# Agent attention and a SoLU feed-forward on one core: the small softmax is transposed two tiles at a time and split into high and low parts behind the transpose

## The chip, the cores and the metric

The kernel runs on one core of one Trainium2 chip. A core has TensorE (PE, matrix products, with a separate weight load PEld), VectorE (DVE), ScalarE (ACT), GpSimd (POOL), and SyncE (SP), whose queue issues all DMAs of this kernel. They run side by side, each through its own list of instructions in a fixed order, and wait for one another by semaphores. The metric is the device time of one execution in microseconds; the time before is the median of three.

## What is computed

Four batches of 12608 rows of 128 columns go through an agent attention with 49 agents and then, all rows together, through a feed-forward of width 1024:

```python
def sm(a, b):
    s = scale * (a @ b.transpose(0, 2, 1))
    e = np.exp(s - s.max(-1, keepdims=True))
    return e / (e.sum(-1, keepdims=True) + 1e-09)
agent_v = sm(agents, k) @ v
x = (sm(q, agents) @ agent_v).reshape(B * S, D)
h = x @ w_in
e = np.exp(h - max(h)); solu = h * e / (sum(e) + 1e-09)
ln = (solu - mean(solu)) / np.sqrt(var(solu) + 1e-06) * g_ln
return ln @ w_out
```

## The kernel before

The rows are cut into 396 tiles of 128, 99 to a batch. Three kinds of work run mixed.

**The agent pass** of a batch (`phase_a`) goes over keys and values in 13 chunks and ends with two matrices `mh` and `ml`, the high and the low part of agent_v times w_in. It runs beside the tiles of the batch before it, so the last batch has none beside it; that of the first batch stands alone at the start, together with the unpacking of the weights.

**The small softmax** of the queries over the 49 agents (`phase_b`) takes units of eight tiles, and in them groups of up to four: 25 groups in a batch, 24 of four tiles and one of three. TensorE makes the logits (`b0`, L647), DVE and ACT turn them into exponentials and the reciprocal of their sum (`b1` to `b3r`). Then, for each group, `b4` on POOL multiplies (L676), copies the result rounded to the fp32r format into columns 0 to 48 of the tile's 128 columns of `pack` (L678), and puts the rest, the low part, into columns 64 to 112 (L680). `b5` transposes each tile's 128 columns by itself into a PSUM bank (L687), and `b6` on ACT copies the bank into `pT` (L692). In `pT` the high part lies in rows 0 to 48 and the low part in rows 64 to 112; `mh` and `ml` hold the same rows twice, so one product takes both parts.

**The tile loop**: `c_h` multiplies a tile's 128 columns of `pT` with `mh` and `ml` into one of two double banks `ph` (L730, four matmuls a tile); DVE takes the maximum (`c_max`, L734), ACT the exponential (`c_exp`, L744), DVE the product with h (`c_u`, L749), ACT the squares (`c_sq`, L755). `c_t` transposes the 1024 columns of the result in two halves of four (L762). A half is then split into a high and a low part in one of two ways: where the table `DIR` (by tile number modulo four, and half) says direct, ACT writes the high part (L777) and DVE subtracts it from PSUM (L786); otherwise ACT copies the half to `uT` (L781) and POOL makes both parts (L790, L794). The last two tiles are direct throughout. `c_w` makes the last product for two tiles at once in 24 matmuls (L810). POOL computes the scale of four tiles (`c_rstd`), which DMAs take to DRAM (`dr`, four small ones, L851) and back to all partitions (`rB`, L852); `c_fin` on DVE multiplies with it (L875) and `c_out` stores (L891).

**What sets the order.** `Plan` is a list scheduler that runs when the program is built: each piece of work is an `op` with an engine, an assumed duration, a due time in tiles and the pieces that it needs; the planner gives the engine that can start first the piece due first among those that can start at about that time. The due times are tile numbers plus constants (`BD0` to `DWL`). The planner's order is fixed for TensorE, ACT, DVE and POOL (the last loop of the kernel); SP's is not, and follows from the tile framework. Transposes, logits, agent products and last products share four PSUM banks `px`: `take` takes one, `free` names the piece after which it is given back. `pT` has eight buffers (`PTB`), each of the two `pack` one.

Of the kernel before, what the change touches and what calls it, by code (L numbers as in the profile page):

```python
# [9 lines left out]
F32 = mybir.dt.float32  # L10
F32R = mybir.dt.float32r
# [3 lines left out]
ALU = mybir.AluOpType  # L15
# [10 lines left out]
class Plan:  # L26
# [15 lines left out]
    def op(self, eng, fn, cost, due, deps=(), take=False, free=None, after=(), kind=1, shy=0.0):  # L42
        o = Op()
        o.kind, o.shy = kind, shy
        o.eng, o.fn, o.cost, o.due, o.take, o.free = eng, fn, cost, due, take, free
        o.deps, o.outs, o.end, o.bank = [d for d in deps if d is not None], [], None, None
        o.left = 0
        for d in o.deps + [d for d in after if d is not None]:
            if d.end is None:
                o.left += 1  # L50
                d.outs.append(o)
        if not o.left:
            self.push(o)
        return o
# [71 lines left out]
def kernel(  # L126
# [11 lines left out]
    nc = tc.nc  # L138
    B, C, N = qT.shape
    A = agT.shape[2]  # L140
    DF = w_in.shape[1]
    P = 128
    NF = DF // P
    HW = 512
    GT = 4
# [3 lines left out]
    AP2 = 64  # L149
    ETE = "AD"  # L150
    CPR = -1.98
    UTB = 4
    DIR = {(1, 0), (1, 1), (3, 1)}
    LGC = 8
    UB = 8
    TD = 2
    WC = 4

    BD0 = 13.69
    BD1 = 15.3  # L160
    BD2 = 9.96
    BD3 = -17.37
    BD4 = 0.17
    BD5 = 5.85
    DH = -3.24
    DMX = -8.66
    DEX = 0.61
    DU_ = -1.62
    DSQ = 20.92
    DT = -0.42  # L170
    DEV = -8.39
    DLD = 1.53
    DSP = -1.16
    DW = 3.3
    DR = 1.58
    DF_ = 5.14
    OUTD = -5.86
    OUTC = -74.58
# [4 lines left out]
    VLAG = 0.25  # L183
    PTB = 8
    SHY = -2.99
    DHR = -4.68
    DHL = -5.42
    DMXR = 10.02
    DMXL = 15.46
# [11 lines left out]
    DLDL = 26.96  # L201
    DSPR = -6.09
    DSPL = 14.43
    DWR = 2.46
    DWL = -0.21
    RBL = 6.0
    ASTART = -3.67
# [6 lines left out]
    const = ctx.enter_context(tc.tile_pool(name="const", bufs=1))  # L214
# [3 lines left out]
    bpool = ctx.enter_context(tc.tile_pool(name="bpool", bufs=2))  # L218
# [8 lines left out]
    ident = const.tile([P, P], F32, name="ident")  # L227
# [118 lines left out]
        ycol.append(yc)  # L346
    packs = []
    for i in range(2):
        pk = const.tile([P, GT, P], F32, name=f"pack{i}")
        nc.gpsimd.memset(pk, 0.0)  # L350
        packs.append(pk)
    logits = []
# [10 lines left out]
    op = plan.op  # L363
# [4 lines left out]
    n = len(seq)  # L368
# [247 lines left out]
    BT, B0, B4, B5, BQ, pT_op, grp_h = {}, {}, {}, {}, {}, {}, {}  # L616

    def col0(t):
        return min(t * P, N - P)
# [12 lines left out]
    groups = []  # L632

    def phase_b(k, dues, gate=()):

        b, t0, nt = units_b[k]
        r = {}
        nq = (nt + GT - 1) // GT

        def b0(j0, j1, px=None):  # L640
            if px is not None:
                r["px"] = px
            qt, px = qts[k], r["px"]
            for j in range(j0, j1):
                for h in range(0, P, AP2):
                    o = col0(t0 + j) - col0(t0) + h
                    nc.tensor.matmul(px[h : h + AP2, j * A : (j + 1) * A], qt[:, o : o + AP2], ag_sb[:, b, :A],  # L647
                                     start=True, stop=True)
            r["lg"] = px[:, : nt * A].rearrange("p (t a) -> p t a", a=A)

        def b1():
            r["mx"] = tiny.tile([P, UB], F32, tag="mx", name=f"mx{b}_{t0}")
            nc.vector.tensor_reduce(out=r["mx"][:, :nt], in_=r["lg"], op=ALU.max, axis=AX.X)

        def b1s():
            mx, lg = r.pop("mx"), r.pop("lg")
            r["e"] = logits[k % 2][:, :nt, :]
            r["d"] = r["e"][:, :, :A]
            nc.vector.tensor_tensor(out=r["d"], in0=lg, in1=mx[:, :nt].unsqueeze(2).to_broadcast([P, nt, A]),
                                    op=ALU.subtract)  # L660

        def b2():
            nc.scalar.activation(out=r["d"], in_=r["d"], func=AF.Exp, scale=SCALE)

        def b3():
            r["s"] = tiny.tile([P, UB], F32, tag="sm", name=f"sm{b}_{t0}")[:, :nt]
            nc.vector.tensor_reduce(out=r["s"], in_=r["e"], op=ALU.add, axis=AX.X)

        def b3r():
            nc.vector.reciprocal(out=r["s"], in_=r["s"])  # L670

        def b4(q):
            m = min(GT, nt - q * GT)
            sl = slice(q * GT, q * GT + m)
            pk, dv = packs[q], r["d"][:, sl, :]
            nc.gpsimd.tensor_tensor(out=dv, in0=dv, in1=r["s"][:, sl].unsqueeze(2).to_broadcast([P, m, A]),  # L676
                                    op=ALU.mult)
            nc.gpsimd.tensor_scalar(out=pk[:, :m, :A].bitcast(F32R), in0=dv, scalar1=1.0, scalar2=0.0,  # L678
                                    op0=ALU.mult, op1=ALU.add)
            nc.gpsimd.tensor_tensor(out=pk[:, :m, AP2 : AP2 + A].bitcast(F32R), in0=dv, in1=pk[:, :m, :A],  # L680
                                    op=ALU.subtract)

        def b5(q, px):
            m = min(GT, nt - q * GT)
            r["pt", q] = px
            for j in range(m):
                nc.tensor.transpose(px[:, j * P : (j + 1) * P], packs[q][:, j, :], ident)  # L687

        def b6(q):
            m = min(GT, nt - q * GT)  # L690
            pT = pTs[b, t0 // GT + q] = bpool.tile([P, GT * P], F32R, tag="pT", bufs=PTB, name=f"pT{b}_{t0}_{q}")
            nc.scalar.copy(out=pT[:, : m * P], in_=r.pop(("pt", q))[:, : m * P])  # L692

        shy = SHY if k < 4 else 0.0
        chunks = [(j, min(j + LGC, nt)) for j in range(0, nt, LGC)]
        prev, first = None, None
        for j0, j1 in chunks:
            f = (lambda px, j0=j0, j1=j1: b0(j0, j1, px)) if prev is None else (lambda j0=j0, j1=j1: b0(j0, j1))
            o = op("P", f, 0.155 * (j1 - j0), dues[0] + 0.1 * j0,
                   [BQ[k], prev, B0.get(k - 1)] + [B4.get((k - 2, q)) for q in range(2)] + list(gate), take=prev is None, kind=2, shy=shy)  # L700
            first = first or o
            prev = o
        B0[k] = prev
        d1 = op("D", b1, 0.047 + 0.0532 * nt, dues[1], [prev], shy=shy)
        d2 = op("D", b1s, 0.05 + 0.0532 * nt, dues[1] + 0.1, [d1] + [B4.get((k - 2, q)) for q in range(2)], free=first, shy=shy)
        a1 = op("A", b2, 0.098 + 0.0402 * nt, dues[2], [d2])
        d3 = op("D", b3, 0.05 + 0.0532 * nt, dues[3], [a1], shy=shy)
        d5 = op("D", b3r, 0.12, dues[3] + 0.2, [d3])
        for q in range(nq):
            g = len(groups)  # L710
            groups.append((b, t0 // GT + q))
            sc = min(GT, nt - q * GT) / GT
            old = B5.get((k - 1, q)) or B5.get((k - 2, q))
            B4[k, q] = op("G", lambda q=q: b4(q), 0.07 + 1.5 * sc, dues[4] + 2.5 * q, [d5, old])
            B5[k, q] = op("P", lambda px, q=q: b5(q, px), 0.435 * sc, dues[5] + 2.5 * q,
                          [B4[k, q], grp_h.get(groups[g - PTB]) if g >= PTB else None], take=True, shy=shy)
            pT_op[groups[g]] = op("A", lambda q=q: b6(q), 0.48 * sc, dues[5] + 2.5 * q + 0.3, [B5[k, q]], free=B5[k, q], shy=shy)
        if k + 2 < nu and k + 2 > 1:
            qload(k + 2, dues[0], [prev])

# [41 lines left out]
            nc.tensor.transpose(pt[:, kf * P : (kf + 1) * P], us[x][0][:, k0 * P : (k0 + 1) * P], ident)  # L762

    def direct(x, hf):
        return (x % GT, hf) in DIR or x >= n - TD

    def parts(x, k0, k1):
        i, j = divmod(x, 2)
# [162 lines left out]
    for x in range(n):  # L931
        b, t = seq[x]
        G, j = divmod(x, GT)
        i = x // 2
        if t % UB == 0:
            first = x
            dues = [first - z for z in (BD0, BD1, BD2, BD3, BD4, BD5)] if ku else [-99.5 + 0.05 * z for z in range(6)]
            phase_b(ku, dues, [] if ku < 2 else [mlast[0]] if ku < 4 else [])
            ku += 1
        for hf in range(2):  # L940
            H[x, hf] = op("P", F(c_h, x, hf), 0.468, at(x, DH, DHR, DHL) + 0.02 * hf,
                          [pT_op[b, t // GT], U.get(x - 2)] + mdone[b][: hf + 1], kind=0)
        grp_h[b, t // GT] = last_h[b] = H[x, 1]
        MX[x] = op("D", F(c_max, x), 1.13, at(x, DMX, DMXR, DMXL), [H[x, 0], H[x, 1]])
        EX[x] = op("A", F(c_exp, x), 1.11, at(x, DEX, DEXR, DEXL), [MX[x], U.get(x - 2), RB.get(G - 3)] + (cout if x < 2 else []))
# [40 lines left out]
        if j == GT - 1:  # L986
# [74 lines left out]
```

## Time and profile before

| | us |
|---|---|
| runs shown | 1573.73, 1576.07, 1573.48; median 1573.73 |
| the profiled execution | 1575.81 |
| its span, first to last instruction | 1574.0 |
| granted TensorE clock | 0.999 of full |
| first L730 (first product of the tile loop) | 64.9 |
| idle of DVE's L734 for TensorE's L730 | 53.3 |
| idle of POOL's L790 for ACT's L781 | 84.6 |

The profile shows one execution. The page gives each engine's busy time and its share of the span, and groups of instructions by line with count, busy time, mean duration and the idle time of the engine ahead of them. The chain of work that ended last goes back from the last instruction, at each step to what released it; its shares by line say where the time goes. A wait is put down to what came last. TensorE's matmuls overlap by a part of their length, so the length of one is read from the pieces of the chain, not from its row.

### The profile page before, as it was taken

How to read it: one execution, taken by the hardware profiler on the slowest of the kernel's cores; microseconds unless marked ns; L12 is line 12 of the kernel's file. 1: busy time of each engine (PE TensorE's matmuls, PEld its weight loads, DVE VectorE, ACT ScalarE, POOL GpSimd, SP SyncE). 2: the span in 40 equal slices, each digit the busy share in tenths (PEclk: the TensorE clock that was granted, in tenths of full speed). 3: DMA queues.
4: the chain of work that ended last, by engine and by line, in shares of the span. 5: the costliest groups of instructions: out<-in, count | busy, mean ns of one | idle time of the engine just before them, and what ended most of it. 6: DMA issues, size and time to landing. Idle time of an engine off the chain costs nothing.

```text
span 1574.0 us, 35069 instructions
## 1 busy us (share of the span) xinstructions
PE 1550.8 (99%) x12821; PEld 1381.7 (88%) x12821; DVE 1376.5 (87%) x2161; ACT 1440.1 (91%) x2740; POOL 1254.5 (80%) x1715
## 2 busy tenths in 40 slices
PE   8899999999999999999999999999999999999998
PEld 5588898998889899898899899898988989999998
DVE  6989898888998888889898888988888998989986
ACT  3599999999999999999999998999989999999996
POOL 2577888888788788787888878887878889988896
PEclk9999999999999999999999999999999999999999
DMA  9422323313123223222222232222111121111111
GB/s 370 150 88 81 96 81 95 95 59 103 62 82 100 82 88 105 91 81 74 88 68 88 88 102 88 88 88 87 49 63 53 47 69 55 62 55 49 45 42 40
DMA packets 57629, 133.65 MB, mean 85 GB/s; under 512 B 9840, under 2 KB 14064, under 8 KB 57456
## 3 DMA queue, kind: packets, MB, share of 16 engines
q1 hardware_dynamic: 57456, 131.41, 26.2%
q8 instruction: 101, 1.65, 0.4%
q14 instruction: 72, 0.59, 0.1%
HBM read 105.36 MB, written 26.02 MB: 83 GB/s over the span
## 4 chain that ended last, share of the span: by engine, by line
PE 89%; DVE 4%; ACT 3%; POOL 2%; issue 1%; DMA 0%; SPq 0%; DVEq 0%; ACTq 0%; POOLq 0%
PE px L810 33%; PE ph L730 22%; PE px L762 21%; PE px L647 3%; PE px L467 3%; PE px L418 3%; PE px L687 3%; PE px L451 1%; ACT e L744 1%; DVE u L749 1%; ACT sq L755 1%; DVE nm L734 1%; POOL uL L794 0%; ACT uT L781 0%; DVE mxp L423 0%
## 5 line engine op out<-in xcount | busy, mean ns | idle before, releaser
L794 POOL TENSOR_TENSOR uL<-uT,uH 128x1024 fp32r<-128x1024 f32 (+1 forms) x295 | 598.6, 2029 | 24.3
L734 DVE TENSOR_REDUCE nm<-ph 128x1 f32<-128x1024 f32 x396 | 480.3, 1219 | 55.3 <-PE ph L730 53.3
L749 DVE SCALAR_TENSOR_TENSOR u<-ph,e 128x1024 f32<-128x1024 f32 x396 | 481.0, 1219 | 54.2 <-ACT e L744 30.3
L755 ACT ACTIVATE sq<-u,su 128x1024 bf16<-128x1024 f32 x396 | 464.0, 1172 | 25.9 <-DVE u L749 22.8
L744 ACT ACTIVATE e<-ph,nm 128x1024 f32<-128x1024 f32 x396 | 446.3, 1132 | 28.4 <-DVE nm L734 25.0
L810 PE MATMUL px<-uL,wH 128*128 128x256 f32 x1584 | 467.2, 295 | 0.1
L810 PE MATMUL px<-uH,wH 128*128 128x256 f32 x1584 | 453.5, 286 | 2.6 <-DVE uL L786 1.4
L810 PE MATMUL px<-uH,wL 128*128 128x256 f32 x1584 | 449.4, 284 | 0.0
L762 PE MATMUL px<-ident,u 128*128 128x128 f32 x3168 | 429.4, 274 | 2.6 <-DVE u L749 0.7
L762 PEld LDWEIGHTS px<-ident,u 128*128 128x128 f32 x3168 | 355.6, 141 | 51.5 <-issue 18.7
L790 POOL TENSOR_SCALAR uH<-uT 128x1024 fp32r<-128x1024 f32 (+1 forms) x295 | 268.3, 909 | 85.7 <-ACT uT L781 84.6
L730 PE MATMUL ph<-mh,pT 128*128 128x512 f32 x792 | 326.3, 412 | 0.7 <-DVE u L749 0.4
L810 PEld LDWEIGHTS px<-uH,wH 128*128 128x128 f32 x1584 | 299.7, 189 | 15.4 <-issue 3.8
L730 PE MATMUL ph<-ml,pT 128*128 128x512 f32 x792 | 312.4, 394 | 0.0
L810 PEld LDWEIGHTS px<-uH,wL 128*128 128x128 f32 x1584 | 300.2, 189 | 9.6
L810 PEld LDWEIGHTS px<-uL,wH 128*128 128x128 f32 x1584 | 299.8, 189 | 9.0 <-issue 4.6
L781 ACT COPY uT<-px 128x512 f32<-128x512 f32 x492 | 272.9, 594 | 13.7 <-issue 3.0
L786 DVE TENSOR_TENSOR uL<-px,uH 128x512 fp32r<-128x512 f32 x300 | 200.9, 681 | 28.0 <-ACT uH L777 27.7
L777 ACT CAST uH<-px 128x512 fp32r<-128x512 f32 x300 | 170.1, 603 | 2.9 <-PE px L762 2.6
L730 PEld LDWEIGHTS ph<-mh,pT 128*128 128x128 f32 x792 | 149.2, 188 | 22.6 <-DVE u L749 4.6
L730 PEld LDWEIGHTS ph<-ml,pT 128*128 128x128 f32 x792 | 149.7, 189 | 17.1 <-DVE ml L543 0.2
L829 POOL TENSOR_TENSOR y<-x,nhalf 128x4 f32<-128x4 f32 x99 | 100.1, 1011 | 7.5
(119 smaller groups left out, 1469.2 us busy)
## 6 DMA issues: line engine op xcount, KB each, us to landing
rB<-dr SPq DMA_DIRECT2D x98, 256.0 KB
qt<-in_qT_dram SPq DMA_DIRECT2D x48, 512.0 KB
out_dram<-ob SPq DMA_DIRECT2D x95, 256.0 KB
kt<-in_kT_dram SPq DMA_DIRECT2D x36, 512.0 KB
vt<-in_v_dram SPq DMA_DIRECT2D x36, 512.0 KB
dr<-yr SPq DMA_DIRECT2D x392, 0.5 KB
kh<-in_kT_dram SPq DMA_DIRECT2D x12, 512.0 KB
vh<-in_v_dram SPq DMA_DIRECT2D x12, 512.0 KB
```

The source lines that it names most:

```text
L730: nc.tensor.matmul(ph[:, sl], lhs, bmats[b]["mh" if m == 0 else "ml"][:, sl], start=(m == 0), stop=(m == 1))
L734: nc.vector.tensor_reduce(out=nms[x], in_=phs[x], op=ALU.max, axis=AX.X, negate=True)
L744: nc.scalar.activation(out=es[x], in_=phs[x], func=AF.Exp, bias=nms.pop(x), accum_out=st[G]["S"][:, j : j + 1])
L749: nc.vector.scalar_tensor_tensor(out=u, in0=phs[x], scalar=INV, in1=es[x], op0=ALU.mult, op1=ALU.mult, accum_out=su)
L755: nc.scalar.activation(out=sq, in_=u, func=AF.Square, bias=su, scale=-float(DF), accum_out=st[G]["Q"][:, j : j + 1])
L762: nc.tensor.transpose(pt[:, kf * P : (kf + 1) * P], us[x][0][:, k0 * P : (k0 + 1) * P], ident)
L777: nc.scalar.copy(out=uH, in_=pt)
L781: nc.scalar.copy(out=rr[x][:, hf * 4 : hf * 4 + 4, :], in_=pt)
L786: nc.vector.tensor_tensor(out=uL, in0=pt, in1=uH.bitcast(F32), op=ALU.subtract)
L790: nc.gpsimd.tensor_scalar(out=uH, in0=rr[x][:, k0:k1, :], scalar1=1.0, scalar2=0.0, op0=ALU.mult, op1=ALU.add)
L794: nc.gpsimd.tensor_tensor(out=uL, in0=rr[x][:, k0:k1, :], in1=uH.bitcast(F32), op=ALU.subtract)
L810: nc.tensor.matmul(po, wt[:, kf, :], ut[:, kf, :], start=(q == 0), stop=(q == WM - 1))
```

## The change

`pack` has 64 columns a tile in place of 128, and `b4` is one multiplication on POOL that writes into it. `b5` transposes two tiles at once, so the even tile's probabilities come out in rows 0 to 48 of the bank and the odd tile's in rows 64 to 112, and a group of four needs 256 columns of the bank. `b6` on ACT copies them, rounded to fp32r, into a new SBUF tile `pn`; the new `b7` on DVE subtracts that from the bank and writes the low part beside it. The new `b8` issues four DMAs on SP that bring the parts to their rows of `pT`: for the even tiles the high part to rows 0 to 63 and the low part to rows 64 to 127, for the odd tiles the other way round. `DIR` is now by tile number modulo eight, with 5 of 16 halves direct in place of 6. The planner gets the new pieces and new constants.

```diff
-    DIR = {(1, 0), (1, 1), (3, 1)}
+    DIR = {(1, 0), (1, 1), (3, 1), (5, 1), (7, 1)}
...
-    BD1 = 15.3
+    BD1 = 8.27
...
-        pk = const.tile([P, GT, P], F32, name=f"pack{i}")
+        pk = const.tile([P, GT, AP2], F32, name=f"pack{i}")
...
-            nc.gpsimd.tensor_tensor(out=dv, in0=dv, in1=r["s"][:, sl].unsqueeze(2).to_broadcast([P, m, A]),
-                                    op=ALU.mult)
-            nc.gpsimd.tensor_scalar(out=pk[:, :m, :A].bitcast(F32R), in0=dv, scalar1=1.0, scalar2=0.0,
-                                    op0=ALU.mult, op1=ALU.add)
-            nc.gpsimd.tensor_tensor(out=pk[:, :m, AP2 : AP2 + A].bitcast(F32R), in0=dv, in1=pk[:, :m, :A],
-                                    op=ALU.subtract)
+            nc.gpsimd.tensor_tensor(out=packs[q][:, :m, :A], in0=r["d"][:, sl, :],
+                                    in1=r["s"][:, sl].unsqueeze(2).to_broadcast([P, m, A]), op=ALU.mult)
...
-            for j in range(m):
-                nc.tensor.transpose(px[:, j * P : (j + 1) * P], packs[q][:, j, :], ident)
+            for j in range(0, m, 2):
+                nc.tensor.transpose(px[:, j * AP2 : (j + 2) * AP2], packs[q][:, j : j + 2, :].rearrange("p j a -> p (j a)"),
+                                    ident)
...
         def b6(q):
+            w = (min(GT, nt - q * GT) + 1) // 2 * P
+            r["n", q] = bpool.tile([P, 2, GT // 2 * P], F32R, tag="pn", bufs=2, name=f"pn{b}_{t0}_{q}")
+            nc.scalar.copy(out=r["n", q][:, 0, :w], in_=r["pt", q][:, :w])
+
+        def b7(q):
+            w = (min(GT, nt - q * GT) + 1) // 2 * P
+            pn = r["n", q]
+            nc.vector.tensor_tensor(out=pn[:, 1, :w], in0=r.pop(("pt", q))[:, :w], in1=pn[:, 0, :w].bitcast(F32),
+                                    op=ALU.subtract)
+
+        def b8(q):
             m = min(GT, nt - q * GT)
+            pn = r.pop(("n", q))
             pT = pTs[b, t0 // GT + q] = bpool.tile([P, GT * P], F32R, tag="pT", bufs=PTB, name=f"pT{b}_{t0}_{q}")
-            nc.scalar.copy(out=pT[:, : m * P], in_=r.pop(("pt", q))[:, : m * P])
+            to = pT.rearrange("a (g i p) -> a g i p", i=2, p=P)
+            for i in range(2):
+                w = (m + 1 - i) // 2
+                r0 = i * AP2
+                for part in range(2):
+                    r1 = r0 if part == 0 else AP2 - r0
+                    nc.sync.dma_start(out=to[r1 : r1 + AP2, :w, i, :].bitcast(F32),
+                                      in_=pn[r0 : r0 + AP2, part, : w * P].rearrange("a (g p) -> a g p", p=P).bitcast(F32))
...
-            pT_op[groups[g]] = op("A", lambda q=q: b6(q), 0.48 * sc, dues[5] + 2.5 * q + 0.3, [B5[k, q]], free=B5[k, q], shy=shy)
+            a6 = op("A", lambda q=q: b6(q), 0.25, dues[5] + 2.5 * q + 0.3, [B5[k, q], pT_op[groups[g - 2]] if g > 1 else None], shy=shy)
+            d7 = op("D", lambda q=q: b7(q), 0.33, dues[5] + 2.5 * q + 0.6, [a6], free=B5[k, q], shy=shy)
+            pT_op[groups[g]] = op("S", lambda q=q: b8(q), (0.24, 0.13 if k else 0, 2.5), dues[5] + 2.5 * q + 0.6,
+                                  [d7, grp_h.get(groups[g - PTB]) if g >= PTB else None], shy=shy)
...
     def direct(x, hf):
-        return (x % GT, hf) in DIR or x >= n - TD
+        return (x % (2 * GT), hf) in DIR or x >= n - TD
```

The lines behind the change are numbered higher: L682 is the transposes of `pack`, L688 and L693 the copy and the subtraction into `pn`, L706 the DMAs, L747 the first product (before: L730), L779 the transposes of u (L762), L827 the last product (L810), L868 and L869 `dr` and `rB` (L851, L852), L908 the store (L891).

TensorE, at the first tile of a unit in the third batch (`pT_8_0` is the unit's first group of four tiles, `pack_112` the pack of its second). Before, it reads:

```order
L762 MATMUL px_124<-ident,u_11777 128x128 x4
L810 MATMUL px_125<-uL_11564,wH 128x256
L810 MATMUL px_125<-uH_11563,wL 128x256
L810 MATMUL px_125<-uH_11563,wH 128x256
L810 MATMUL px_125<-uL_11564,wH 128x256
L687 MATMUL px_126<-ident,pack_112 128x128 x4
L730 MATMUL ph_122<-mh_11199,pT_8_0_11688 128x512
L730 MATMUL ph_122<-ml_11200,pT_8_0_11688 128x512
```

Four transposes fill a bank there. In the changed kernel the pack of the first group (`pack_110`) is transposed here, some 20 rows ahead of the first product with that group:

```order
L747 MATMUL ph_123<-ml_11321,pT_0_1_11603 128x512
L682 MATMUL px_126<-ident,pack_110 128x128 x2
L747 MATMUL ph_123<-mh_11320,pT_0_1_11603 128x512
L747 MATMUL ph_123<-ml_11321,pT_0_1_11603 128x512
L827 MATMUL px_127<-uH_11706,wH 128x256
L827 MATMUL px_127<-uL_11707,wH 128x256
L827 MATMUL px_127<-uH_11706,wL 128x256
L827 MATMUL px_127<-uH_11706,wH 128x256
L467 MATMUL px_125<-vt_0_11810,eT_0_11968 64x128 x8
L779 MATMUL px_124<-ident,u_11853 128x128 x4
L779 MATMUL px_126<-ident,u_11934 128x128 x4
L779 MATMUL px_125<-ident,u_11934 128x128 x4
```

Two transposes stand where four stood. Behind these rows come eight of L827, the pair for `pack_112`, and then the first L747 that reads `pT_8_0_11994`.

SP at the same unit. Before, its queue has the scales, the stores and the loads (`qt`, `kt`, `vt` are queries, keys, values):

```order
L851 DMA dr_11974<-yr_11972 4x32 x4
L407 DMA vt_3_12028<-in_v_dram 128x1024
L852 DMA rB_11975<-dr_11974 128x512
L891 DMA out_dram<-ob_12132 128x512
L627 DMA qt_40_12176<-in_qT_dram 128x1024
```

Now the four transfers of each group stand among them:

```order
L627 DMA qt_32_11847<-in_qT_dram 128x1024
L908 DMA out_dram<-ob_11837 128x512
L868 DMA dr_11888<-yr_11882 4x32 x4
L396 DMA kt_2_11920<-in_kT_dram 128x1024
L396 DMA kt_3_11937<-in_kT_dram 128x1024
L869 DMA rB_11889<-dr_11888 128x512
L706 DMA pT_8_0_11994<-pn_8_0_11972 64x2x128 x4
L407 DMA vt_2_12011<-in_v_dram 128x1024
L868 DMA dr_12044<-yr_12038 4x32 x4
L706 DMA pT_8_1_12092<-pn_8_1_12068 64x2x128 x3
L869 DMA rB_12045<-dr_12044 128x512
L706 DMA pT_8_1_12092<-pn_8_1_12068 64x2x128
```

`pT_8_0_11994` goes out only behind the `rB` in front of it, which waits until its four `dr` have landed, and the last transfer of `pT_8_1_12092` behind another.

More of the change, by code (lines that the diff above doesn't have):

```diff
@@ L159 @@
     BD0 = 13.69
-    BD1 = 15.3
+    BD1 = 8.27
     BD2 = 9.96
-    BD3 = -17.37
-    BD4 = 0.17
+    BD3 = -18.57
+    BD4 = 0.41
     BD5 = 5.85
[L165 to L169, printed above, removed]
-    DT = -0.42
[L171 to L175, printed above, removed]
+    DH = -3.05
+    DMX = -3.31
+    DEX = 7.76
+    DU_ = 6.48
+    DSQ = 21.68
+    DT = -0.42
+    DEV = -6.42
+    DLD = 1.96
+    DSP = 2.68
+    DW = 3.31
+    DR = 2.33
     DF_ = 5.14
@@ L185 @@
     SHY = -2.99
-    DHR = -4.68
+    DHR = -4.59
     DHL = -5.42
@@ L203 @@
     DSPL = 14.43
-    DWR = 2.46
+    DWR = 0.63
     DWL = -0.21
@@ L674, in b4 @@
             sl = slice(q * GT, q * GT + m)
-            pk, dv = packs[q], r["d"][:, sl, :]
-            nc.gpsimd.tensor_tensor(out=dv, in0=dv, in1=r["s"][:, sl].unsqueeze(2).to_broadcast([P, m, A]),
-                                    op=ALU.mult)
-            nc.gpsimd.tensor_scalar(out=pk[:, :m, :A].bitcast(F32R), in0=dv, scalar1=1.0, scalar2=0.0,
-                                    op0=ALU.mult, op1=ALU.add)
-            nc.gpsimd.tensor_tensor(out=pk[:, :m, AP2 : AP2 + A].bitcast(F32R), in0=dv, in1=pk[:, :m, :A],
-                                    op=ALU.subtract)
+            nc.gpsimd.tensor_tensor(out=packs[q][:, :m, :A], in0=r["d"][:, sl, :],
+                                    in1=r["s"][:, sl].unsqueeze(2).to_broadcast([P, m, A]), op=ALU.mult)
         def b5(q, px):
@@ L713, in phase_b @@
             old = B5.get((k - 1, q)) or B5.get((k - 2, q))
-            B4[k, q] = op("G", lambda q=q: b4(q), 0.07 + 1.5 * sc, dues[4] + 2.5 * q, [d5, old])
-            B5[k, q] = op("P", lambda px, q=q: b5(q, px), 0.435 * sc, dues[5] + 2.5 * q,
-                          [B4[k, q], grp_h.get(groups[g - PTB]) if g >= PTB else None], take=True, shy=shy)
-            pT_op[groups[g]] = op("A", lambda q=q: b6(q), 0.48 * sc, dues[5] + 2.5 * q + 0.3, [B5[k, q]], free=B5[k, q], shy=shy)
+            B4[k, q] = op("G", lambda q=q: b4(q), 0.08 + 0.53 * sc, dues[4] + 2.5 * q, [d5, old])
+            B5[k, q] = op("P", lambda px, q=q: b5(q, px), 0.218, dues[5] + 2.5 * q, [B4[k, q]], take=True, shy=shy)
+            a6 = op("A", lambda q=q: b6(q), 0.25, dues[5] + 2.5 * q + 0.3, [B5[k, q], pT_op[groups[g - 2]] if g > 1 else None], shy=shy)
+            d7 = op("D", lambda q=q: b7(q), 0.33, dues[5] + 2.5 * q + 0.6, [a6], free=B5[k, q], shy=shy)
+            pT_op[groups[g]] = op("S", lambda q=q: b8(q), (0.24, 0.13 if k else 0, 2.5), dues[5] + 2.5 * q + 0.6,
+                                  [d7, grp_h.get(groups[g - PTB]) if g >= PTB else None], shy=shy)
         if k + 2 < nu and k + 2 > 1:
```

## The prediction

> **What bounds the kernel now.** I read first the busy shares, then the chain of work that ended last, cut into stretches (each answer opens with the chain's shares by line), then the chain's pieces in one ordinary stretch. A busy share only says who could be the limit.
>
> ```profile
> PE 1550.8 (99%) x12821; PEld 1381.7 (88%) x12821; DVE 1376.5 (87%) x2161; ACT 1440.1 (91%) x2740; POOL 1254.5 (80%) x1715
> by line: PE px L810 37.3%; PE ph L730 25.0%; PE px L762 23.6%; PE px L467 4.1%; PE px L418 4.0%; PE px L687 2.6%; PE px L647 2.1%; PE px L451 1.4%
> by line: PE px L810 34.6%; PE ph L730 23.1%; PE px L762 22.7%; PE px L467 3.4%; PE px L647 3.3%; PE px L418 3.2%; PE px L687 2.8%; PE px L451 1.4%; ACT e L744 0.7%; DVE nm L734 0.7%; issue 0.6%; DVE u L749 0.6%; ACT sq L755 0.4%; ACT uT L78
> by line: PE px L810 30.6%; PE ph L730 21.4%; PE px L762 19.5%; PE px L647 3.6%; ACT e L744 3.4%; issue 3.1%; ACT sq L755 2.7%; PE px L687 2.5%; POOL uL L794 2.3%; ACT uT L781 1.8%; DVE u L749 1.6%; ACT uH L777 1.4%; DVE nm L734 1.1%; POOL u
> by line: PE px L810 43.8%; PE ph L730 24.1%; PE px L762 24.0%; PE px L687 2.4%; PE px L647 2.1%; PE px L862 0.7%; ACT rB L866 0.3%; issue 0.2%; DVE ob L875 0.2%; ACT pT L692 0.2%
> ```
>
> The four chain rows are 100 to 200, 200 to 1190, 1190 to 1400 and 1400 to 1574 us. TensorE's lines add up to 100%, 94.5%, 78% and 97%: outside the first 100 us the kernel goes at TensorE's pace, except in the third stretch, where a fifth of the chain lies on the other engines. The transposes that the change halves (L687) are on the chain everywhere: 2.6 + 27.7 + 5.3 + 4.2 = 39.8 us of it.
>
> ```profile
> 616.37 0.44 PE px L762 x4
> 616.81 0.47 PE px L810 x4
> 617.28 0.44 PE px L687 x4
> 617.72 0.92 PE ph L730 x4
> 620.62 0.89 PE px L467 x16
> ```
>
> The pieces are start, length, engine and line. TensorE goes from piece to piece without a gap; a transpose costs 0.44/4 = 0.11 us, a matmul of L810 0.117, of L730 0.23, of L467 0.056.
>
> ```profile
> 400.00:600.00 200.00, 199.02 (x1661) 178.05 (x1660) 176.59 (x276) 186.75 (x354) 160.15 (x223) 1.00 0.27 85
> 1200.00:1400.00 200.00, 198.41 (x1661) 183.58 (x1660) 182.78 (x274) 196.57 (x367) 172.87 (x243) 1.00 0.18 57
> ```
>
> Columns: stretch, length, then busy us of PE, PEld, DVE, ACT, POOL, granted clock, DMA share, GB/s. Up to about 1190 us ACT has 7% left; after it, with no agent pass left to mix in, ACT is at 98%, DVE at 91%.
>
> **The change, part by part.** All rows below: busy us and mean ns of one.
>
> ```profile
> L687 PE MATMUL px<-ident,pack 128*128 128x128 f32 x396 | 59.8, 273 | 1.2 <-POOL pack L680 0.6 <-ACT uT L781 0.6
> L692 ACT CAST pT<-px 128x512 fp32r<-128x512 f32 x96 | 57.7, 601 | 6.0 <-PE px L687 5.8
> L692 ACT CAST pT<-px 128x384 fp32r<-128x384 f32 x4 | 2.0, 496 | 0.0
> L678 POOL TENSOR_SCALAR pack<-logits 128x196 fp32r<-128x196 f32 x96 | 34.5, 360 | 8.4
> L680 POOL TENSOR_TENSOR pack<-logits,pack 128x196 fp32r<-128x196 f32 x96 | 55.3, 576 | 8.0
> L786 DVE TENSOR_TENSOR uL<-px,uH 128x512 fp32r<-128x512 f32 x300 | 200.9, 681 | 28.0 <-ACT uH L777 27.7
> L659 DVE TENSOR_TENSOR logits<-px,mx 128x392 f32<-128x392 f32 x48 | 27.1, 565 | 1.2
> ```
>
> TensorE: there are 100 groups (96 of four tiles, 4 of three). 396 transposes become 96x2 + 4x2 = 200, so 196 x 0.11 = 21.6 us go. 39.8 of L687's 43.6 us lie on the chain, so **-20 us** at the end.
>
> ACT: the eviction shrinks from 512 to 256 columns. From 601 and 496 ns the slope is 0.82 ns a column, so 0.39 us: 100 x 0.21 = 21 us off ACT. That matters in the third stretch: with ACT as short of time as TensorE, the relief must come on both, and does. I count it nowhere a second time.
>
> DVE: 100 new subtractions of 256 columns out of PSUM; from 681 and 565 ns for 512 and 392 columns the slope is 0.97, so 0.43 us, 43 us in all. The table of directly split halves goes from 300 to 251, which takes 49 x 0.681 = 33 us off. Net +10 us on 1376: hidden under TensorE's 99%; without that cover it is 10 us at the end. In the first 100 us, where DVE is on the chain, two of the new subtractions stand before the mean of the weights: **+1 us**.
>
> ```profile
> L794 POOL TENSOR_TENSOR uL<-uT,uH 128x512 fp32r<-128x512 f32 x98 | 126.1, 1287 | 8.0
> L790 POOL TENSOR_SCALAR uH<-uT 128x512 fp32r<-128x512 f32 x98 | 60.9, 621 | 4.2 <-ACT uT L781 4.1
> L810 PE MATMUL px<-uL,wH 128*128 128x256 f32 x1584 | 467.2, 295 | 0.1
> ```
>
> POOL loses the split of the packed probabilities, 100 x (0.360 + 0.576) = 94 us, and gains the 49 halves, 49 x (0.621 + 1.287) = 93 us. Net nothing; but one half per eight tiles now comes 1.9 us behind its eviction by POOL, not 0.7 by DVE. TensorE idled 0.1 us before the matmuls that read this result, so they come well after it: cost 0, and if that cover were gone up to 49 x 1.2 = 59 us.
>
> SP: 400 new DMAs, each waiting for the ACT copy or the DVE subtraction of its group.
>
> ```profile
> 609.80 1.27 SPq L851 DMA_DIRECT2D dr<-yr  x4
> 612.01 0.35 SPq L852 DMA_DIRECT2D rB<-dr  x1
> 1170.39 3.15 DMA qt<-in_qT_dram
> SPq L627 <- PE px L647: 86.3, 33, 8.8
> q1 hardware_dynamic: 57456, 131.41, 26.2%
> ```
>
> Four issues take 1.27 us, 0.32 each: 128 us on a queue that spends the time waiting. The engines behind it are 26% busy, and 26 MB more on 131 stay far from full. What counts is the **latency L** from the transposes to the first L730 that reads the group. It was eviction alone. Now it is transposes 0.22, copy 0.39, subtraction 0.43, two issues 0.64 (the first tile needs only the first pair of DMAs) and the landing. No row shows an SBUF to SBUF transfer; the nearest are the four small ones, landed 612.01 - 611.07 = 0.94 us after the last issue, and the q load on the chain, 3.15 us for up to 512 KB. So L is 2.6 to 4.8 us with nobody in front. What stands in front is an instruction of up to 1.2 us on ACT and on DVE, and on SP an rB that waits for its four (2.2 us from 609.80 to 612.01): up to 9.4 us. All engines but SP are 80 to 90% busy, so I take the middle, **L = 6**.
>
> Against this stands TensorE's own work between the two places in the new order. Priced with the pieces above, the row that the order shows for pT_8_0_11994 comes 4.1 us after its transposes began; six more groups have 5.0, 5.3, 5.4, 5.9, 5.9 and 6.3 us, the next 8.5; the other first halves of a unit 8.6 to 11.7, the second halves 12 to 17. At L = 6 the seven stall for 1.9 + 1.0 + 0.7 + 0.6 + 0.1 + 0.1 = **4 us**; at 2.6 for nothing, at 9.4 for 28 us plus about 2 for the next ones. Behind a waiting L730 stands all of TensorE, and so everyone.
>
> The bank of a group is freed by the subtraction, not by the copy: 0.4 us longer on one of four banks, once in 15 us. I cost it at nothing, since the planner lets a stage take a bank only when it is free by its times, and counts this; uncovered it would be 0.4 x 100 = 40 us. Waits on several DMAs add semaphore instructions ahead of matmuls; those exist now too:
>
> ```profile
> L810 PEldq EVENT_SEMAPHORE  x64: 51/51/51, 76.7 to 1564.3; - x64
> ```
>
> 64 of 51 ns stand before L810, of which the row quoted above idles for 0.1 us: hidden, since the queue runs ahead.
>
> Sum: -20 + 4 + 1 = -15 us. The profiled execution took 1575.8 us (span 1574.0 and 1.8 around it), so 1560.8; the median shown is 2.1 lower, so **1558.7 us**.
>
> Four issues landed within 2.2 us of the first one here, so transfers overlap. The Trainium skill, "DMA: Bandwidth & Descriptors", section "Rules for kernel authors", speaks against this form: two transfers to disjoint partition halves are not worth it, since they serialize, and under 64 KB one pays mostly overhead. These are four of 64 KB in halves. With the roughly 2 us fixed per DMA that its section on the anatomy of one DMA gives for another issuing path, four in a row would be 8 us, L an estimated 9.5 and the sum about +11 instead of -15. The quartet at 609.80 disagrees, though it is far smaller; a late landing is the second rival, with a chance from rows.
>
> **The rivals.**
> 1. *The freed time is not used.* The pair's matmuls now wait for POOL's later half, or DVE (89% of the new time) delays the next stage. For it: the third stretch, where a fifth of the chain is not TensorE. Against: 0.1 us of idle before L810. Price: a quarter of the 1.2 us at 49 places is 15 us, all that the sum leaves: 1574 us.
> 2. *The transfers come late* (the slower side). SP is one queue in a fixed order, and the new DMAs stand behind loads that wait for TensorE (86.3 us in 33 waits for the q loads alone, up to 8.8). If L reaches 9.4, the stalls are 30 us and the sum -20 + 30 + 1 = +11: 1585 us. It decides from L = 8.5, where the seven places lose about 21 us. Against: the order puts the q load's release about 8.9 us before the L730 concerned.
> 3. *The re-planned order is better by itself.* All due times moved; the third stretch has 22% of 210, 47 us of chain off TensorE. A quarter of that gained would give 1547 us.
> 4. That the transposes are not halved is excluded by the order.
>
> **How the numbers follow.** Forecast 0.58 (1553 to 1568), better order 0.10 (1543 to 1553), half of the gain lost 0.08 (1568 to 1570.5), rival 1 0.10 (1570.5 to 1577), rival 2 0.14 (above 1577, to 1600). A measurement can tell about 0.2%, 3 us, from no change. Faster by more: 0.58 + 0.10 + 0.08 = 0.76; within 0.10; slower 0.14. The range 1546 to 1580 leaves out the tails of rival 2 and of the better order, under 0.2.
>
> **What would show it.** Right: transposes at 200 with the same length of one, L687's successor at half its share of the chain, ACT's copy near 0.39 us, POOL's total unchanged, DVE 10 us up. Wrong: idle time before L730's successor put down to a DMA of pT, above all at the seven places; waits of the px matmuls for POOL's uL; a landing of pT over 3 us; ACT or DVE taking over the chain before 1190 us.

## The result, and the profile after

The changed kernel takes 1549.33 us, the median of four runs (1548.65 to 1550.09); the kernel before takes 1574.24 us beside it (1573.48 to 1576.07). The ratio is 0.9838 with a 95% interval of 0.9826 to 0.985: 25 us or 1.6% faster, 9 us more than forecast.

The page of the changed kernel, its busy shares, its DMA queue, and its chain by engine; the last row is the chain of the kernel before:

```profile
PE 1526.4 (99%) x12628; PEld 1356.1 (88%) x12628; DVE 1372.4 (89%) x2214; ACT 1421.6 (92%) x2738; POOL 1252.9 (81%) x1613
q1 hardware_dynamic: 114544, 157.39, 34.0%
PE 95%; DVE 3%; ACT 1%; DMA 1%; issue 0%; SPq 0%; DVEq 0%; ACTq 0%
PE 89%; DVE 4%; ACT 3%; POOL 2%; issue 1%; DMA 0%; SPq 0%; DVEq 0%; ACTq 0%; POOLq 0%
```

All shares are close to those before. What changed is the chain: TensorE holds 95% of it, where it held 89%. The chain by line in two stretches, the later agent passes (200 to 1170 us) and the first half of the last batch (1170 to 1375 us), answers to the second and third row of the prediction:

```profile
by line: PE px L827 37.0%; PE ph L747 24.4%; PE px L779 23.6%; PE px L467 3.6%; PE px L647 3.5%; PE px L418 3.3%; PE px L682 1.4%; PE px L451 1.4%; DMA pT<-pn 0.4%; PE px L531 0.4%; issue 0.2%; DMA dr<-yr 0.1%; DVE nm L751 0.1%; DVE uL L803
by line: PE px L827 40.7%; PE ph L747 27.0%; PE px L779 26.3%; PE px L647 3.7%; PE px L682 1.6%; PE px L531 0.8%; PE px L523 0.1%
```

L682 has half of L687's share beside the agent passes, as it should. The second row is the surprise: in the first half of the last batch, where 22% of the chain lay off TensorE before, none does now.

The new and changed groups, as count, busy us and mean ns, then SP's row for the transfers (shortest, median and longest issue in ns):

```profile
L682 PE MATMUL px<-ident,pack 128*128 128x128 f32 x200 | 38.2, 273 | 0.1
L688 ACT CAST pn<-px 128x256 fp32r<-128x256 f32 x100 | 37.9, 380 | 4.2 <-PE px L682 3.6
L693 DVE TENSOR_TENSOR pn<-px,pn 128x256 fp32r<-128x256 f32 x100 | 41.9, 419 | 5.2 <-ACT pn L688 4.8
L803 DVE TENSOR_TENSOR uL<-px,uH 128x512 fp32r<-128x512 f32 x251 | 168.8, 685 | 47.5 <-ACT uH L794 45.8
L811 POOL TENSOR_TENSOR uL<-uT,uH 128x512 fp32r<-128x512 f32 x147 | 189.6, 1290 | 12.2
L706 SPq DMA_DIRECT2D pT<-pn x400: 590/599/1925, 41.5 to 1516.5; - x134
```

To see where the 25 us lie, the kernel is cut at the first matmul of each batch's `mh` and `ml` (agent_v times w_in, L531). One such row of each kernel in the timeline, before and then changed:

```profile
425.24 1.02 PE L531 MATMUL px<-win_sb,av_dup 128*128 128x512 f32 x2
```

```profile
418.21 1.02 PE L531 MATMUL px<-win_sb,av_dup 128*128 128x512 f32 x2
```

These two are those of the second batch. Stages in us, each from one profiled execution, for the kernels of this document; "start" ends at the first product of the tile loop, the next three hold an agent pass beside the tiles, the last has none and ends with the last matmul:

| kernel | start | 1st | 2nd | 3rd | last | median of runs |
|---|---|---|---|---|---|---|
| before | 64.9 | 360.3 | 382.6 | 384.2 | 378.5 | 1574.2 |
| changed | 62.2 | 356.0 | 377.6 | 378.5 | 368.4 | 1549.3 |
| e3 new form, old numbers | 64.4 | 355.5 | 378.4 | 377.8 | 384.5 | 1566.4 |
| e5 changed, old table | 62.1 | 358.4 | 376.9 | 378.9 | 374.4 | 1556.4 |
| e4 old form, new numbers | 64.8 | 360.1 | 384.6 | 383.8 | 393.8 | 1591.6 |
| e7 old form, new due times | 65.3 | 359.2 | 382.0 | 385.1 | 384.0 | 1580.7 |
| e1 pairs twice | 62.4 | 360.5 | 382.3 | 383.1 | 373.2 | 1566.5 |
| e2 ACT longer | 61.6 | 358.9 | 380.6 | 381.3 | 373.1 | 1562.3 |
| e8 VectorE longer | 63.2 | 359.4 | 380.4 | 381.2 | 371.6 | 1560.6 |
| e9 no subtraction | 61.4 | 356.9 | 377.6 | 378.1 | 367.8 | 1549.7 |
| e10 GpSimd longer | 61.6 | 356.7 | 377.6 | 379.4 | 368.7 | 1550.3 |
| e6 transfers twice | 62.2 | 364.0 | 377.4 | 407.0 | 370.7 | 1583.5 |
| e12 fewer direct halves | 62.6 | 358.2 | 386.0 | 384.8 | 367.9 | 1567.0 |

The three stages with an agent pass give 4.3 + 5.0 + 5.7 = 15.0 us, the last batch 10.1, the start 2.7.

### The profile page after: what moved, and what is told of

Same layout as the page of the kernel before. It is cut to its first block, busy times and chain, and to the rows that moved or that the text cites. A ratio compares the mean times of both kernels' runs of the same rounds, so it can differ in the third digit from the quotient of the medians.

```text
span 1546.9 us, 35512 instructions
## 1 busy us (share of the span) xinstructions
PE 1526.4 (99%) x12628; PEld 1356.1 (88%) x12628; DVE 1372.4 (89%) x2214; ACT 1421.6 (92%) x2738; POOL 1252.9 (81%) x1613
## 4 chain that ended last, share of the span: by engine, by line
PE 95%; DVE 3%; ACT 1%; DMA 1%; issue 0%; SPq 0%; DVEq 0%; ACTq 0%
PE px L827 36%; PE ph L747 24%; PE px L779 23%; PE px L647 3%; PE px L467 3%; PE px L418 3%; PE px L451 1%; PE px L682 1%; PE px L531 0%; DMA pT<-pn 0%; DVE mxp L423 0%; DVE nm L751 0%; DMA kh<-in_kT_dram 0%; DVE ca_in L263 0%; DVE uL L803 0%
## 5 line engine op out<-in xcount | busy, mean ns | idle before, releaser
L811 POOL TENSOR_TENSOR uL<-uT,uH 128x1024 fp32r<-128x1024 f32 (+1 forms) x344 | 661.5, 1923 | 27.6
L827 PE MATMUL px<-uL,wH 128*128 128x256 f32 x1584 | 466.9, 295 | 0.2 <-POOL uL L811 0.2
L827 PE MATMUL px<-uH,wH 128*128 128x256 f32 x1584 | 450.6, 284 | 1.8 <-DVE uL L803 1.8
L827 PE MATMUL px<-uH,wL 128*128 128x256 f32 x1584 | 448.1, 283 | 0.0
L779 PE MATMUL px<-ident,u 128*128 128x128 f32 x3168 | 425.5, 274 | 2.7 <-DVE uL L803 1.4
L779 PEld LDWEIGHTS px<-ident,u 128*128 128x128 f32 x3168 | 356.7, 141 | 55.2 <-issue 20.7
L807 POOL TENSOR_SCALAR uH<-uT 128x1024 fp32r<-128x1024 f32 (+1 forms) x344 | 298.3, 867 | 98.4 <-ACT uT L798 98.0
L747 PE MATMUL ph<-mh,pT 128*128 128x512 f32 x792 | 329.7, 416 | 1.6 <-DMA pT<-pn 1.3
L827 PEld LDWEIGHTS px<-uH,wH 128*128 128x128 f32 x1584 | 299.0, 189 | 16.9 <-issue 3.5
L747 PE MATMUL ph<-ml,pT 128*128 128x512 f32 x792 | 312.3, 394 | 0.0
L798 ACT COPY uT<-px 128x512 f32<-128x512 f32 x541 | 299.2, 589 | 11.9 <-PE px L779 3.0
L827 PEld LDWEIGHTS px<-uH,wL 128*128 128x128 f32 x1584 | 299.1, 189 | 8.6 <-issue 0.7
L827 PEld LDWEIGHTS px<-uL,wH 128*128 128x128 f32 x1584 | 298.9, 189 | 8.5 <-issue 4.6
L803 DVE TENSOR_TENSOR uL<-px,uH 128x512 fp32r<-128x512 f32 x251 | 168.8, 685 | 47.5 <-ACT uH L794 45.8
L747 PEld LDWEIGHTS ph<-mh,pT 128*128 128x128 f32 x792 | 149.3, 188 | 20.3 <-issue 3.4
L747 PEld LDWEIGHTS ph<-ml,pT 128*128 128x128 f32 x792 | 149.9, 189 | 17.7 <-issue 0.5
L794 ACT CAST uH<-px 128x512 fp32r<-128x512 f32 x251 | 143.7, 592 | 1.2 <-PE px L779 0.9
```

What stands on the lines that cost most here:

```text
L747: nc.tensor.matmul(ph[:, sl], lhs, bmats[b]["mh" if m == 0 else "ml"][:, sl], start=(m == 0), stop=(m == 1))
L794: nc.scalar.copy(out=uH, in_=pt)
L798: nc.scalar.copy(out=rr[x][:, hf * 4 : hf * 4 + 4, :], in_=pt)
L803: nc.vector.tensor_tensor(out=uL, in0=pt, in1=uH.bitcast(F32), op=ALU.subtract)
L807: nc.gpsimd.tensor_scalar(out=uH, in0=rr[x][:, k0:k1, :], scalar1=1.0, scalar2=0.0, op0=ALU.mult, op1=ALU.add)
L811: nc.gpsimd.tensor_tensor(out=uL, in0=rr[x][:, k0:k1, :], in1=uH.bitcast(F32), op=ALU.subtract)
```

## The experiments

Eleven kernels ran; each has its row in the table above. Their ratios below are to the kernel before, run beside them (medians of 1573.65 to 1575.04 us), with 95% intervals. A difference of 1 or 2 us between kernels of different experiments is not read as one.

**e1: the saved transposes put back.**

```diff
-            for j in range(0, m, 2):
+            for j in [j for j in range(0, m, 2) for _ in range(2)]:
```

> The changed kernel, but each transpose of two tiles is issued twice into the same place: TensorE gets back the 200 x 0.11 = 22 us that the change took off it, nothing else moves. Theory A (the gain is TensorE's freed time, since TensorE sets the pace): about 1549 + 20 to 22 = 1569 to 1571 us. Rival B (the gain comes from the re-planned order and the new table of direct halves): at most 1549 + 5 = 1554 us. Rival C (the gain is ACT's shorter eviction): at most 1552 us.

Measured 1566.5 us, ratio 0.9948 (0.9933 to 0.9962): 17.2 us more than the changed kernel, spread evenly over the stages (4.5, 4.7, 4.6, 4.8). TensorE's time is paid at about four fifths of its length. Rivals B and C fall as the whole story.

**e2: ACT's saving put back.** A small copy ahead of the eviction; ACT's busy time goes from 1421.6 to 1439.7 us.

```diff
+            nc.scalar.copy(out=r["n", q][:, 0, :64], in_=r["pt", q][:, :64])
             nc.scalar.copy(out=r["n", q][:, 0, :w], in_=r["pt", q][:, :w])
```

> The changed kernel, but ACT first copies 64 columns of the bank to the place that it then overwrites: about 0.22 us more of ACT for each of the 100 groups, what the change took off ACT. Theory A: hidden while the agent pass runs beside (ACT has 6% left there), and up to 26 x 0.22 = 6 us in the last batch: 1549 to 1555 us. Rival C (ACT's shorter eviction is the gain): 1549 + 22 = 1571 us. Rival B: no change, 1549 us.

Measured 1562.3 us, ratio 0.9927 (0.991 to 0.9943): 13 us for 18 us of ACT, and not only in the last batch (4.7) but in each stage beside an agent pass too (2.9, 3.0, 2.8). My theory missed: ACT's idle time, 8% of the span in the changed kernel, did not hide it. The chain of e2 from 200 to 1170 us shows how:

```profile
by line: PE px L828 31.5%; PE ph L748 21.0%; PE px L780 20.2%; PE px L647 3.1%; PE px L467 3.0%; PE px L418 3.0%; issue 2.5%; ACT sq L773 2.5%; ACT e L762 1.6%; DVE nm L752 1.5%; ACT uT L799 1.3%; PE px L451 1.3%; DVE u L767 1.2%; PE px L68
```

The lines are those of the changed kernel, moved by one. TensorE's share of this stretch has dropped from 99% to 85%, and links of ACT (squares, exponential, copy) and VectorE (maximum, u) have come in. I read this as the tile loop's own circle, from the product over maximum, exponential and u back to the two `ph` banks, with ACT's other work in between. The copy also delays the transfers, but TensorE's idle time for them is only 2.6 us in e2, where it is 1.3 in the changed kernel. The 17 us of e1 and the 13 of e2 are together more than the 25 that the change gained, so these prices are not shares of the gain; both together were not tried.

**e3 and e4: form and numbers taken apart.** e3 is the new form with all due times and the table of the kernel before; e4 the old form with those of the changed kernel.

```diff
-    DIR = {(1, 0), (1, 1), (3, 1), (5, 1), (7, 1)}
+    DIR = {(1, 0), (1, 1), (3, 1)}
...
-    BD1 = 8.27
+    BD1 = 15.3
...
-        return (x % (2 * GT), hf) in DIR or x >= n - TD
+        return (x % GT, hf) in DIR or x >= n - TD
```

(e3 against the changed kernel, with all other due times in the same way; e4 is the reverse on the kernel before.)

> The changed kernel with all due times and the table of direct halves (6 of 16) of the kernel before. Theory A: the gain stays but for what the order adds, 1549 + 3 to 8 = 1552 to 1557 us. Rival B: the gain is gone, 1570 us or more.

> The kernel before with all due times and the table of direct halves (5 of 16) of the changed one. Theory A: no gain, 1570 to 1580 us. Rival B: most of the gain, 1550 to 1558 us.

Measured 1566.4 (0.9948, 0.9933 to 0.9963) and 1591.6 us (1.0107, 1.0092 to 1.0122). Both theories miss in both runs, and the stages say where. Beside the agent passes e3 gains 4.8 + 4.2 + 6.4 = 15.4 us on the kernel before, all that the changed kernel has there, whatever the numbers. But its last batch is 6.0 us longer than before. In e4 little changes beside the agent passes (1.4 us more in all), and the last batch is 15.3 us longer. For e4 the busy shares point to GpSimd:

```profile
PE 1558.2 (98%) x12821; PEld 1381.4 (87%) x12821; DVE 1349.1 (85%) x2114; ACT 1441.9 (91%) x2738; POOL 1348.4 (85%) x1813
```

GpSimd has the packed split and the 49 more halves at once, 94 to 96 us more than in the two kernels. So the numbers alone are no gain; they belong to the form.

**e5 and e7: the table taken apart from the due times.** e5 is the changed kernel with only the old table, e7 the kernel before with only the new due times.

```diff
-    DIR = {(1, 0), (1, 1), (3, 1), (5, 1), (7, 1)}
+    DIR = {(1, 0), (1, 1), (3, 1)}
...
-        return (x % (2 * GT), hf) in DIR or x >= n - TD
+        return (x % GT, hf) in DIR or x >= n - TD
```

(e5; e7 is e4 without its two lines on the table.)

> The changed kernel with only the table of direct halves put back (6 of 16, by tile number modulo four); the due times are the changed kernel's. Theory A2 (beside the agent passes the new form saves about 5 us a batch whatever the order; the last batch depends on how the split halves are shared between VectorE and GpSimd): the last batch loses about 10 us or more, 1559 to 1567 us in all. Rival D (the due times, not the table, make the last batch): within 3 us of the changed kernel, 1549 to 1552 us.

> The kernel before with the changed kernel's due times but its own table of direct halves (6 of 16). Theory A2: the 16 us that the old form lost with both came from GpSimd, which had the packed split and the 49 more halves at once, so without the new table it is within 5 us of the kernel before, 1571 to 1580 us. Rival D: it stays near 1590 us.

Measured 1556.4 (0.9889, 0.9874 to 0.9904) and 1580.7 us (1.0045, 1.0028 to 1.0062). e5 loses 7 us, 6.0 of them in the last batch, so the table is worth 6 us there in the new form; that is less than the 10 that theory A2 named and more than the 3 of rival D, so both missed. e7 gets 11 of e4's 17 us back and stays 6.5 above the kernel before, just outside theory A2's range; rival D is out. For the old form the new table costs 11, the new due times 6.5. From e3 to e5, the due times are worth 10 us to the new form. A new table also gives the planner another order, so each of these figures is that of the numbers with the order that follows from them.

**e8, e9 and e10: is VectorE or GpSimd tight?** e8 adds a subtraction of 64 columns ahead of the new one (busy time of VectorE 1372.4 to 1391.6 us), e9 leaves the subtraction out (the low part is then the high part a second time), e10 adds a copy on GpSimd (1252.9 to 1289.0 us).

```diff
+            nc.vector.tensor_tensor(out=pn[:, 1, :64], in0=r["pt", q][:, :64], in1=pn[:, 0, :64].bitcast(F32),
+                                    op=ALU.subtract)
             nc.vector.tensor_tensor(out=pn[:, 1, :w], in0=r.pop(("pt", q))[:, :w], in1=pn[:, 0, :w].bitcast(F32),
```

> The changed kernel with VectorE first subtracting 64 columns into the place that it then overwrites: about 0.23 us more for each of 100 groups, 23 us. Theory A2 (TensorE and ACT are the two tight engines, VectorE at 89% has room): at most 5 us slower, 1549 to 1554 us. Rival F (all four engines are tight, and any 22 us on one costs 13 to 17 us, as on TensorE and ACT): 1562 us or more.

```diff
         def b7(q):
-            w = (min(GT, nt - q * GT) + 1) // 2 * P
-            pn = r["n", q]
-            nc.vector.tensor_tensor(out=pn[:, 1, :w], in0=r.pop(("pt", q))[:, :w], in1=pn[:, 0, :w].bitcast(F32),
-                                    op=ALU.subtract)
+            r.pop(("pt", q))
...
-                                      in_=pn[r0 : r0 + AP2, part, : w * P].rearrange("a (g p) -> a g p", p=P).bitcast(F32))
+                                      in_=pn[r0 : r0 + AP2, 0, : w * P].rearrange("a (g p) -> a g p", p=P).bitcast(F32))
```

> The changed kernel without the new subtraction on VectorE: the low part is not computed, and the transfers take the high part to both places, so the output is not the reference's; the order of everything else stays. It takes 100 x 0.42 = 42 us off VectorE. The prediction's step (VectorE's added work is hidden): within 3 us, 1546 to 1550 us. Theory F (work on any engine costs about half to four fifths of its length): 15 us or more faster, 1534 us or less. In between, the relief of an engine is worth less than its burden costs.

```diff
+            nc.gpsimd.tensor_scalar(out=packs[q][:, :m, :A], in0=r["d"][:, sl, :], scalar1=1.0, scalar2=0.0,
+                                    op0=ALU.mult, op1=ALU.add)
             nc.gpsimd.tensor_tensor(out=packs[q][:, :m, :A], in0=r["d"][:, sl, :],
```

> The changed kernel with GpSimd first copying the exponentials of a group to the place that it then overwrites: 100 x 0.36 = 36 us more on GpSimd, a good third of the 94 us that the change took off it. Theory F: 13 to 20 us slower, 1562 to 1570 us. Its rival (only the chain TensorE, VectorE, ACT of the tile loop is tight, GpSimd with 19% idle has room): at most 5 us slower, most of it in the last batch, where GpSimd is at 90%.

Measured 1560.6 (0.9916, 0.9901 to 0.9931), 1549.7 (0.9839, 0.9824 to 0.9854) and 1550.3 us (0.9848, 0.9832 to 0.9864). 19 us put on VectorE cost 11, so theory A2 missed and F was nearer; but all 100 subtractions taken away gain nothing, and F's other half falls: the new VectorE work is indeed hidden. (They are 42 us by their lengths, but VectorE's busy time falls by 26 only, since an instruction's record overlaps the next one's.) An engine's burden and its relief are not worth the same here: without the subtractions the loop still goes at TensorE's pace. 36 us on GpSimd cost 1, so F falls there too. The busy shares of e9 and e10:

```profile
PE 1524.3 (99%) x12628; PEld 1355.2 (88%) x12628; DVE 1346.1 (87%) x2114; ACT 1422.9 (92%) x2738; POOL 1255.7 (81%) x1613
```

```profile
PE 1525.8 (99%) x12628; PEld 1355.5 (88%) x12628; DVE 1373.5 (89%) x2214; ACT 1422.5 (92%) x2738; POOL 1289.0 (83%) x1713
```

TensorE is at 99% in both.

**e6: the transfers made later.** Every group's four transfers go out a second time behind the first.

```diff
-            for i in range(2):
+            for i in (0, 1, 0, 1):
```

> The changed kernel with each group's four transfers issued a second time behind the first, with the same bytes: SP gets 400 x 0.6 = 240 us more and a group's rows are there 2.5 to 4 us later. Theory A2 (the transfers have slack): up to 4 us slower, at the few places with little TensorE work in between, 1549 to 1553 us. Rival E (the transfers are near the path everywhere): 99 groups x 1 us or more each for half of them, 1600 us and above.

Measured 1583.5 us, ratio 1.0062 (1.0045 to 1.008): 34 us slower than the changed kernel. The profiled execution is 38.5 us longer than that of the changed kernel, 28.5 of them in the third stage and 8.0 in the first. Neither theory has this: it is not everywhere, and it is not small. The timeline of e6, all places with over 1 us of TensorE's idle time put down to these transfers (start, length, instruction, idle time before it):

```profile
419.61 0.77 PE L747 MATMUL ph<-mh,pT 128*128 128x512 f32 x1 [3.62 <-DMA pT<-pn]
858.13 0.47 PE L747 MATMUL ph<-mh,pT 128*128 128x512 f32 x1 [3.44 <-DMA pT<-pn]
955.65 0.80 PE L747 MATMUL ph<-mh,pT 128*128 128x512 f32 x1 [4.01 <-DMA pT<-pn]
991.79 0.47 PE L747 MATMUL ph<-mh,pT 128*128 128x512 f32 x1 [2.99 <-DMA pT<-pn]
1027.05 0.77 PE L747 MATMUL ph<-mh,pT 128*128 128x512 f32 x1 [2.86 <-DMA pT<-pn]
1124.02 0.47 PE L747 MATMUL ph<-mh,pT 128*128 128x512 f32 x1 [3.01 <-DMA pT<-pn]
1157.38 0.47 PE L747 MATMUL ph<-mh,pT 128*128 128x512 f32 x1 [1.36 <-DMA pT<-pn]
```

There are seven, one at the end of the first batch and six in the third, and they are the groups with the seven shortest distances in the changed kernel's trace. The rows add up to 21.3 us. Shorter waits of the same kind add 1.8, and one wait for a key load 2.9. Most of the rest is TensorE's clock. Two stretches of e6, behind the third and the seventh row (stretch, length, TensorE's busy us, granted clock, DMA share, GB/s):

```profile
954.70:961.50 6.80, 5.85 (x22) 0.50 0.22 55
1157.40:1160.80 3.40, 3.40 (x31) 1.00 0.19 46
```

At each of the first six rows, with 2.9 to 4.0 us of idle time, the granted clock falls to 0.50 within 1.4 us of the wait's end, for 3.4 or 6.8 us, 27.3 us in all; some 25 of them lie outside the waits, and about half of that is lost, 13 us. At the seventh row, with 1.36 us, the clock stays at 1.00, as it does in the whole of the changed kernel's work. Idle time and clock together make about 37 of the 38.5 us.

The first of the seven is also the only place where the changed kernel itself waits for these transfers. Its timeline there:

```profile
408.52 0.36 SPq L627 DMA_DIRECT2D qt<-in_qT_dram  x1
409.06 0.60 SPq L706 DMA_DIRECT2D pT<-pn  x1
409.83 0.46 SPq L869 DMA_DIRECT2D rB<-dr  x1
410.38 5.67 SPq L706 DMA_DIRECT2D pT<-pn  x7
414.47 0.47 PE L747 MATMUL ph<-mh,pT 128*128 128x512 f32 x1 [1.29 <-DMA pT<-pn]
```

A q load stands in front of the group's first transfer, and an `rB` between the first and the second. (The last SP row merges the other three of this group, issued until 412.28, with the next group's four, from 413.52.) The second transfer, which the first tile needs, begins at 410.38, lands at 414.33 by the trace's semaphore updates, and TensorE starts at 414.47. Read in the same way, the 400 transfers land 2.1 us (median) after their issue began, and the 103 of them that begin within 3 us of a query, key or value load 3.8 us. That is the mechanism of the prediction's second rival, at one place and for 1.3 us.

**e12: a try at a faster version.** Fewer direct halves beside the agent passes, where GpSimd has room.

```diff
+        if x < (B - 1) * TB and x % (2 * GT) == 7:
+            return False
         return (x % (2 * GT), hf) in DIR or x >= n - TD
```

> A try at a faster version: the changed kernel with 4 of 16 halves direct in the first three batches, where GpSimd has room, and 5 of 16 in the last. It takes 37 x 0.685 = 25 us off VectorE and puts 37 x 1.91 = 71 us on GpSimd; the planner makes a new order. Theory F with VectorE's price of 0.58 us per us: up to 14 us faster, 1535 to 1545 us. If GpSimd's relief was itself part of the gain: no gain or slower, 1549 to 1560 us.

Measured 1567.0 us, ratio 0.9951 (0.9937 to 0.9966): 18 us slower than the changed kernel, 8.4 and 6.3 us of it in the second and third stage; both theories missed. GpSimd is at 84%, and e10 shows that busy time alone costs next to nothing there. What is left is that these halves arrive later, or the new order that the planner makes of it; the two were not separated. TensorE's idle time has some of both: 2.9 us for GpSimd's `uL` (0.2 in the changed kernel) and 5.6 for the transfers (1.3). No version here beats the changed kernel.

## Why the prediction came true, and which terms were off

The direction and the range held, the range by 3 us: the time fell not into the forecast's own 1553 to 1568 us but into the case beside it, "the re-planned order is better by itself" (1543 to 1553, a chance of 0.10), and that case is only in part what happened. By the prediction's own steps:

- **TensorE sets the pace: right.** 196 transposes fewer were to give 20 us. The stages beside the agent passes gave 15.0 us, where 75 of the 100 groups at 0.22 us make 16.5, and e3 has the same 15.4 us without the new numbers. e1 gives 17 of 22 back. The form also takes 94 us off GpSimd and shortens ACT's copies; that the 15 us are TensorE's alone rests on its 94.5% of the chain and on e1.
- **The chain's third stretch: the term left out.** The last batch was counted at its share of the 20 us, about 5, and gave 10.1. The step that failed is "cost 0" for the table of direct halves, and with it a sum in which the due times had no term at all: e5 shows 6 us for the table in the last batch, and e3 against e5 10 us for the due times, which again is the last batch (384.5 against 374.4). In place of one gain on one engine, the last batch depends on how ACT, VectorE and GpSimd are fed, and the 22% that lay off TensorE in its first half went away. The third rival had the place and the size, a quarter of 47 us; its mechanism is right only in part, since e4 and e7 show that the new numbers are not better in themselves: in the old form they cost 17 us, or 6.5 without the table.
- **ACT: duration right (0.39 us said, 0.380 measured), weight too small.** The text let ACT count in the third stretch only. e2 shows that 18 us on ACT cost 13, in every stage. This is the price of a burden; what the relief is worth by itself was not measured.
- **VectorE: right.** 0.43 us said, 0.419 measured; instead of 10 us more its busy time is 4 less, since busy time counts only 26 of the subtractions' 42 us, and e9 shows that the added work costs nothing. The cover is thin, as e8 shows.
- **GpSimd: right.** 1254.5 us before, 1252.9 after, and e10 says that it has room.
- **The transfers: the mechanism right, the sizes off.** An issue takes 0.60 us, not 0.32, so SP spends 240 us on them, not 128. The stall was 1.3 us at one place, not 4 at seven, because L = 6 was too long for most groups (the median is 4.5): at six of the seven places the first pair of transfers lands 3.55 to 5.02 us after the transposes began, ahead of 4.7 to 6.6 us of TensorE's work (priced at 4.1 to 6.3); at the seventh it lands after 7.3, against 6.1 of work. Two of the prediction's own signs of being wrong are there, idle time put down to a `pT` transfer and landings over 3 us (121 of 400 from the start of their issue), without being costly. e6 is the test of the second rival: there the first product starts 7.9 to 10.8 us after the transposes began, and 34 us are lost. That this is near the prediction's 30 us for L = 9.4 is partly luck, since about 13 us of it are the lowered clock, which the prediction had not counted.
- **The start: wrong sign.** 1 us more was said, 2.7 less measured (64.9 to 62.2 us). Both kernels with the new form and the new due times start like that (e5 at 62.1), those with only one of them do not (64.4, 64.8, 65.3). Which step of the start it is was not tried.

With the terms as measured, -15.0 for the agent stages, -10.1 for the last batch and -2.7 for the start make -27.8 us in the profiles (spans 1574.0 and 1546.9, with the ends after the last matmul), 25 in the medians. The misses do not cancel: the agent stages gave the 15 us of TensorE without the 4 us of stalls, the last batch 5 more than its share, and the start 3.7 more, all on the faster side.

## What to carry to other kernels

Where one engine holds the chain, count its saved instructions, and expect to be paid about four fifths to all of their time; but cut the chain into stages first, since a stage that is tight on several engines may answer with twice the sum, and the numbers that share work between engines have to move with the change. Test hidden work by taking it away, not by doubling it: 26 us of VectorE's busy time removed gave nothing, 19 us added cost 11. When a wait is moved behind a queue of DMAs, list the distances in the order between producer and consumer: the few short ones are where a later landing will be paid, and here they were counted before the run. In e6 such a wait was paid more than once, as idle time and then as a halved clock.

## What was not expected of the hardware

A DMA of 64 partitions with two runs of 512 bytes in each takes SP 0.60 us to issue (median 599 ns of 400), while the loads, stores and small transfers of the same kernel take 0.29 to 0.36 (medians). Around six waits of 2.9 to 4.0 us in e6, TensorE's granted clock was 0.50 for 3.4 or 6.8 us. It stayed at 1.00 behind the waits of 1.36 us there and 1.29 us in the changed kernel, and once also behind one of 2.9 us, for the key load. Four transfers a group from SBUF to SBUF on disjoint halves, with 2.8 us (median) from the first issue to the landing of the first pair, cost TensorE 1.3 us of idle time in the whole kernel, though the queue's 57,000 further packets raise its share from 26.2% to 34.0%.
